# Attention, MLP and experts on one core: the order of steps where the MLP ends and the experts begin

## Chip, core and metric

The kernel runs on one core of a Trainium2 chip. The metric is device time in microseconds of one execution; lower is better. The numbers of before are three timed executions and one execution taken by the hardware profiler.

## What is computed

A gated linear attention over 4 batches, 8 heads, 768 steps and 48 columns a head gives 3072 tokens of 384 columns. An MLP with a hidden layer of 2048 follows, and then eight experts with a hidden layer of 1024, of which each token goes to the one with the largest logit.

```python
def _attn_ref(q, k, v, f_logit):
    f = 1.0 / (1.0 + np.exp(-f_logit))
    for t in range(S):
        state = f[:, :, t, :, None] * state + np.einsum('bhd,bhe->bhde', k[:, :, t], v[:, :, t])
        y[:, :, t] = np.einsum('bhd,bhde->bhe', q[:, :, t], state)

def _moe_ref(x, w_in, w_out):
    h = x @ w_in
    return (h * (1.0 / (1.0 + np.exp(-h)))) @ w_out

def _moe2_ref(x, w_gate, w1, w2):
    logits = x @ w_gate
    expert_idx = np.argmax(logits, axis=1)
    ...
    for e in range(E):
        mask = expert_idx == e
        h = np.maximum(x[mask] @ w1[e], 0.0)
        out[mask] = gate_w[mask, None] * (h @ w2[e])
```

## The kernel before

Products in float32 are made of three: each operand is split into a rounded high part (a cast, on ScalarE) and a low part (a subtraction, on VectorE), and high x low, low x high and high x high are added up in PSUM. So every weight is loaded as `w_raw` and split into `w_hi` and `w_lo`, and every activation likewise.

Tokens go in chunks of 128 rows and groups of two or three chunks. The MLP runs 128 steps (a group and one of 16 blocks of the hidden layer); a step computes `ph` (L420 in the profile, as all matmuls), evicts it into `sg` (VectorE, L679), splits that into `gh` and `gl`, and adds to the output `px` two steps later. After a group its rows `x` are turned (`plt`), multiplied with the gate (`plg`), the best expert is picked, its rank in the expert is counted (`pr`), and `route` scatters the rows into the DRAM buffer `xs` by an indirect DMA of GpSimd. Each row of `xs` carries 384 columns, the weight and the token's number.

The experts run in the order of their size, found from the counts. Of the first expert, the first 256 slots are the head: `head_fetch` loads them (`xe_h`) before the last groups are scattered, and `head_start` and `turn` prepare them during the last MLP step. The other 256 slots are the rest (`rest_fetch`, `xe_r`, 128 rows each), which must wait until the last scatter has landed. `up` is one of eight blocks of an expert's first layer (nine matmuls, then an eviction on ScalarE, `hh`, and one on VectorE, `hl`); `down` is the second layer for 128 tokens (24 matmuls of 384 columns) and ends in `store`: ScalarE scales the rows into `o`, the token's numbers are cast to integers (`oi`, L987), and GpSimd scatters the rows to the output by these numbers. A tile of `up` is in one of two PSUM banks for even blocks, in one of three for odd ones.

Between the last MLP step and `moe2`, which runs the rest and then the other seven experts, stands the joint. Its order is the string `TAIL`, a letter for each step: `o` the output product of one of the two last MLP steps, `f` the next of ten fill steps (eight `up` and two `down` of the head), `l` the turn of the last group's rows, `m` its logits, `p` and `r` pick and route, `w` (`preload`) the four loads and eight splits of the second expert's first layer, `g` `rest_fetch`, `k` the final ranking of the experts, `t` the turn of the rest (`pxs_r`), `F` what is left of the fill steps.

TensorE runs in program order throughout. On ScalarE, VectorE and GpSimd what is wrapped in `keep` holds its program order and the rest is placed by a scheduler; SP's loads of weights and rows are kept. Each queue works strictly in the order that results.

Of the kernel before, what the change touches and what calls it, by code (L numbers as in the profile page):

```python
# [71 lines left out]
KACT = 7  # L72
ND = 1
MO = 'oeh'
TAIL = 'ofolfmfpfrffwgfkfftF'
FILL_H = 3
HF0 = 137
FX = 0
# [29 lines left out]
HEAD = 2  # L108
# [6 lines left out]
def kernel(  # L115
# [14 lines left out]
    nc = tc.nc  # L130
    B, H, S, D = q.shape
    NT, DM = out.shape
    DFF = moe_w_in.shape[1]
    E, _, F2 = moe2_w1.shape
    KC = DM // P
    NF = DFF // P
    NF2 = F2 // P
# [24 lines left out]
    def bank(kind, name):  # L162
        return ps.tile([P, 512], F32, tag=kind, name=name, bufs={"h": 2, "x": 3, "a": 3}[kind])
# [83 lines left out]
    def keep(fn):  # L247
        return lambda *a, **k: tc.keep_in_program_order(fn(*a, **k))  # L248
# [442 lines left out]
    def moe_o(g, i):  # L691
        hi, lo = gt.pop((g, i))
        first, last = (0,), (NF - 1,)
        wh, wl = units["out", i // 4]
        if i in first:
            px[g] = [
                spare_bank.pop() if (g, t) == (1, 0) else bank("a" if g == 1 else "x", f"px_{g}_{t}")
                for t in range(sizes[g])
            ]
        for t in range(sizes[g]):  # L700
            o = px[g][t][:, :DM]
            m = slice(t * P, (t + 1) * P)
            pe.matmul(o, hi[:, m], wl[:, i % 4, :], start=i in first, stop=False)
            pe.matmul(o, lo[:, m], wh[:, i % 4, :], start=False, stop=False)
            pe.matmul(o, hi[:, m], wh[:, i % 4, :], start=False, stop=i in last)
        if i in last:
            moe_x2(g, i)
# [20 lines left out]
    def logits_pe(g):  # L728
        for t in range(sizes[g]):
            r = x2[starts[g] + t]  # L730
            pt = bank("a", f"plt_{g}_{t}")
            for c in range(KC):
                pe.transpose(pt[:, c * P : (c + 1) * P], r[:, c * P : (c + 1) * P], ident)
            rt = att.tile([P, KC, P], F32, tag="sg", name=f"rt_{g}_{t}", bufs=SG)
            (keep(nc.scalar.copy) if t % 2 < RT - 1 else nc.vector.tensor_copy)(rt.rearrange("p c t -> p (c t)"), pt[:, :DM])
            rts.append(rt)

    def logits_pe2(g):
        for t, rt in enumerate(rts):
            pl = bank(LB, f"plg_{g}_{t}")  # L740
            for c in range(KC):
                pe.matmul(pl[:, :E], rt[:, c, :], wgc[:, c, :E], start=c == 0, stop=c == KC - 1)
            nc.vector.tensor_copy(lgt[g][:, t, :], pl[:, :E])
# [223 lines left out]

        return total

    def down(it, t):  # L970
        e = it["e"]
        po = bank("x", f"po_{it['nm']}_{t}")
        m = slice(t * P, min((t + 1) * P, it["w"]))
        n = m.stop - m.start
        for i in range(NF2):
            hi, lo = it["g", i]
            wh, wl = units["w2", e, i // 4]
            pe.matmul(po[:n, :DM], hi[:, m], wl[:, i % 4, :], start=i == 0, stop=False)
            pe.matmul(po[:n, :DM], lo[:, m], wh[:, i % 4, :], start=False, stop=False)
            pe.matmul(po[:n, :DM], hi[:, m], wh[:, i % 4, :], start=False, stop=i == NF2 - 1)  # L980
        store(it, t, po, n)

    def store(it, t, po, n):
        r = it["rows"](t)
        o, idx = it["out"](t)
        nc.scalar.activation(o[:n], po[:n, :DM], AF.Copy, scale=r[:n, DM : DM + 1])
        nc.vector.tensor_copy(idx[:n], r[:n, DM + 1 : DM + 2])  # L987
        ins = keep(nc.gpsimd.indirect_dma_start)(
            out=out[:, :], out_offset=bass.IndirectOffsetOnAxis(ap=idx[:n], axis=0),
            in_=o[:n], in_offset=None, bounds_check=NT - 1, oob_is_err=False,  # L990
        )
        tc.declare_no_dep(ins.ins, group="outs", reason="each row of out is written by one token")
        tc.add_to_no_dep_group("outs", ins.ins)
# [15 lines left out]
    items = {}  # L1009
# [326 lines left out]
    for n in range(NCH):  # L1336
        g, r = group_of[n]
# [74 lines left out]
    def queue(early):  # L1412
# [3 lines left out]
        f=lambda n: load_chunk(n, "f"), k=lambda n: load_chunk(n, "k"), q=lambda n: load_chunk(n, "q"),  # L1416
# [43 lines left out]
            fn(*args)  # L1460
    g = NG - 1
    outs = seq[total - LAG :]
    ops = [(up, i) for i in range(NF2)] + [(down, t) for t in range(HEAD)]

    def fill(n):
        for fn, i in ops[:n]:
            fn(items["head"], i)
        del ops[:n]

    def preload():  # L1470
# [1 line left out]
            load_expert_unit(("w1", 1, j), nc.vector)  # L1472

    todo = dict(
        o=lambda: moe_o(*outs.pop(0)), f=lambda: fill(1), F=lambda: fill(len(ops)), l=lambda: logits_pe(g),
        m=lambda: logits_pe2(g), p=lambda: pick(g), r=lambda: route(g), w=preload, k=rank_rest,
        g=rest_fetch, t=lambda: turn(items["rest"]),
    )
    for c in TAIL:
        todo[c]()  # L1480
# [47 lines left out]
```

## Time and profile before

| | us |
|---|---|
| three executions | 815.58, 817.85, 818.96 |
| median | 817.85 |
| profiled execution, device time | 820.14 |
| its span, first to last instruction | 818.4 |
| TensorE busy in the span | 799.3 (98%) |
| VectorE, ScalarE, GpSimd busy | 468.1, 378.7, 62.5 |

The span is what the trace covers; the device time of the same execution also has what lies around it. A matmul's end in the trace is modelled and overlaps the next one's start, so TensorE's busy share says where it stands still, and not how fast it is. A row of a timeline is a start, a duration, an engine, a line, an operation, the tiles (output<-inputs) and a count; in brackets is the idle time before it and what ended it.

### The profile page before, as it was taken

The page shows a single profiled execution, that of the slowest core. Times are in us where ns is not written, and L with a number is a line of the kernel's source. Part 1 is how long each engine was busy: PE and PEld are TensorE (multiplying, and loading weights), DVE is VectorE, ACT ScalarE, POOL GpSimd, SP SyncE. Part 2 cuts the span into 40 slices and gives each one's busy share as a digit, 9 for nine tenths or more (in the row PEclk, how much of TensorE's full clock was granted, in tenths as well). Part 3 has the DMA queues.
Part 4 walks back from the last instruction along what each step waited for, and adds up shares of the span by engine and source line. Part 5 has one row for each costly group of instructions (what it writes and reads, how often), then busy time and mean ns, then how long its engine had stood idle before and what let it go on. Part 6 is the DMA issues. An engine that isn't in the chain of part 4 may idle for free.

```text
span 818.4 us, 15643 instructions
## 1 busy us (share of the span) xinstructions
PE 799.3 (98%) x5831; PEld 750.0 (92%) x5831; DVE 468.1 (57%) x1258; ACT 378.7 (46%) x838; POOL 62.5 (8%) x114
## 2 busy tenths in 40 slices
PE   7999999999999999999999999999999999999996
PEld 4889979989999999999999999999998999989996
DVE  6789986555556556556556556366565335256420
ACT  5465564453453463454435343355464436455421
POOL 2000000002000100100100100001200110110011
PEclk9799999999999999999999999999999999999999
DMA  9566586424233343343443321424281528546500
GB/s 213 152 167 167 167 248 188 109 41 116 77 89 80 102 94 87 98 107 79 108 97 78 98 68 40 136 59 127 67 308 56 175 70 270 170 154 213 173 26 30
DMA packets 173197, 100.34 MB, mean 123 GB/s; under 512 B 115507, under 2 KB 166723, under 8 KB 173110
## 3 DMA queue, kind: packets, MB, share of 16 engines
q1 hardware_dynamic: 168724, 88.56, 39.6%
q0 software_dynamic: 3280, 9.49, 3.1%
q10 hardware_dynamic: 1106, 1.18, 0.4%
q8 instruction: 48, 0.79, 0.4%
q14 instruction: 39, 0.32, 0.1%
HBM read 79.35 MB, written 16.97 MB: 118 GB/s over the span
## 4 chain that ended last, share of the span: by engine, by line
PE 74%; issue 8%; DVE 7%; DMA 6%; ACT 3%; SPq 1%; POOL 1%; POOLq 0%; ACTq 0%; DVEq 0%
PE ph L420 21%; PE px L420 20%; PE po L420 7%; PE p L420 7%; PE py L420 3%; PE sc L420 2%; DMA w_raw<-in_moe_w_dram 2%; DVE out_cv L248 1%; PE pyb L420 1%; PE pl L420 1%; PE pq L425 1%; PE plt L425 1%; PE p_r L420 1%; PE pk L425 1%; PE po_r L420 1%
## 5 line engine op out<-in xcount | busy, mean ns | idle before, releaser
L420 PE MATMUL px<-out_lo,gh 128*128 128x384 f32 x368 | 130.2, 354 | 0.0
L679 DVE SCALAR_TENSOR_TENSOR sg<-se,ph 128x384 f32<-128x384 f32 (+1 forms) x113 | 60.1, 532 | 117.1 <-ACT se L677 116.0
L420 PE MATMUL ph<-xth,in_lo 128*128 128x384 f32 (+1 forms) x384 | 123.9, 323 | 1.0 <-DVE sg L679 0.8
L420 PE MATMUL px<-out_hi,gl 128*128 128x384 f32 x368 | 124.0, 337 | 0.0
L420 PE MATMUL ph<-xth,in_hi 128*128 128x384 f32 (+1 forms) x384 | 123.6, 322 | 0.0
L420 PE MATMUL ph<-xtl,in_hi 128*128 128x384 f32 (+1 forms) x384 | 122.3, 325 | 1.3 <-DVE sg L248 1.2
L420 PE MATMUL px<-out_hi,gh 128*128 128x384 f32 x368 | 123.4, 335 | 0.0
L677 ACT ACTIVATE se<-ph 128x384 f32<-128x384 f32 (+1 forms) x113 | 53.6, 474 | 137.6 <-PE ph L420 132.1
L687 ACT CAST gh<-sg 128x384 fp32r<-128x384 f32 (+1 forms) x113 | 56.4, 499 | 52.6 <-DVE sg L679 49.0
L688 DVE TENSOR_TENSOR gl<-sg,gh 128x384 fp32r<-128x384 f32 (+1 forms) x113 | 60.5, 535 | 25.8 <-ACT gh L687 24.0
L420 PEld LDWEIGHTS ph<-xtl,in_hi 128*128 128x128 f32 x384 | 71.7, 188 | 3.0 <-DVE sg L248 1.9
L420 PEld LDWEIGHTS ph<-xth,in_lo 128*128 128x128 f32 x384 | 72.2, 188 | 1.8 <-DVE sg L679 1.1
L420 PEld LDWEIGHTS ph<-xth,in_hi 128*128 128x128 f32 x384 | 72.1, 188 | 0.0
L420 PEld LDWEIGHTS px<-out_lo,gh 128*128 128x128 f32 x368 | 69.1, 188 | 2.5 <-ACT gh L687 0.6
L420 PEld LDWEIGHTS px<-out_hi,gl 128*128 128x128 f32 x368 | 69.3, 188 | 0.3
L420 PEld LDWEIGHTS px<-out_hi,gh 128*128 128x128 f32 x368 | 69.1, 188 | 0.0
L420 PE MATMUL po<-w_lo,hh 128*128 128x384 f32 (+4 forms) x184 | 62.9, 342 | 0.0
L420 PE MATMUL po<-w_hi,hh 128*128 128x384 f32 (+4 forms) x184 | 61.9, 336 | 0.0
L420 PE MATMUL po<-w_hi,hl 128*128 128x384 f32 (+4 forms) x184 | 61.9, 336 | 0.0
L276 DVE TENSOR_TENSOR w_lo<-w_raw,w_hi 128x384 fp32r<-128x384 f32 x104 | 52.5, 552 | 13.2 <-ACT w_hi L275 13.2
L420 PE MATMUL p<-xsl,w_hi 128*128 128x480 f32 (+6 forms) x168 | 58.4, 347 | 0.0
L420 PE MATMUL p<-xsh,w_hi 128*128 128x480 f32 (+6 forms) x168 | 58.3, 347 | 0.0
(290 smaller groups left out, 1532.5 us busy)
## 6 DMA issues: line engine op xcount, KB each, us to landing
w_raw<-in_moe_w_dram SPq DMA_DIRECT2D x64, 384.0 KB
xs<-big SPq DMA_DIRECT2D x8, 776.0 KB
in_again<-in_moe_w_in_dram SPq DMA_DIRECT2D x16, 384.0 KB
out_again<-in_moe_w_out_dram SPq DMA_DIRECT2D x16, 384.0 KB
in_raw<-in_moe_w_in_dram SPq DMA_DIRECT2D x15, 384.0 KB
xe<-xs SPq DMA_DIRECT2D x7, 776.0 KB
out_raw<-in_moe_w_out_dram SPq DMA_DIRECT2D x14, 384.0 KB
f<-in_f_logit_dram SPq DMA_DIRECT2D x24, 192.0 KB
```

The costliest lines, as they stand in the source:

```text
L248: return lambda *a, **k: tc.keep_in_program_order(fn(*a, **k))
L276: (keep(lo_engine.tensor_sub) if pin else lo_engine.tensor_sub)(lo[:, h], x, hi[:, h].bitcast(F32))
L420: ins = nc.tensor.matmul(*a, **k)
L425: ins = nc.tensor.transpose(*a, **k)
L677: ac.activation(e, ph[:, :GT], AF.Tanh, scale=0.5)
L679: ve.scalar_tensor_tensor(out=t, in0=e, scalar=1.0, in1=ph[:, :GT], op0=ALU.add, op1=ALU.mult)
L687: ac.copy(hi, t)
L688: ve.tensor_sub(lo, t, hi.bitcast(F32))
```

## The change

`store` casts the token numbers on GpSimd (`nc.gpsimd.tensor_copy`) in place of VectorE. `down` can run in two parts: its eight blocks are split in two halves for the head's second tile, the first half is the letter `H` and the second half with the store is `F`, and the fill steps are now nine. `TAIL` goes from `ofolfmfpfrffwgfkfftF` to `ofoflfmfpfrfgfkffHtwF`: one `up` step stands between the last `o` and `l`, the rest's turn `t` stands between `H` and `F`, and `w` goes from before `g` to behind `t`.

```diff
@@ -72,7 +72,7 @@
 KACT = 7
 ND = 1
 MO = 'oeh'
-TAIL = 'ofolfmfpfrffwgfkfftF'
+TAIL = 'ofoflfmfpfrfgfkffHtwF'
 FILL_H = 3
 HF0 = 137
 FX = 0
@@ -967,24 +967,27 @@
 
         return total
 
-    def down(it, t):
+    def down(it, t, steps=range(NF2)):
         e = it["e"]
-        po = bank("x", f"po_{it['nm']}_{t}")
+        if steps[0] == 0:
+            it["po", t] = bank("x", f"po_{it['nm']}_{t}")
+        po = it["po", t]
         m = slice(t * P, min((t + 1) * P, it["w"]))
         n = m.stop - m.start
-        for i in range(NF2):
+        for i in steps:
             hi, lo = it["g", i]
             wh, wl = units["w2", e, i // 4]
             pe.matmul(po[:n, :DM], hi[:, m], wl[:, i % 4, :], start=i == 0, stop=False)
             pe.matmul(po[:n, :DM], lo[:, m], wh[:, i % 4, :], start=False, stop=False)
             pe.matmul(po[:n, :DM], hi[:, m], wh[:, i % 4, :], start=False, stop=i == NF2 - 1)
-        store(it, t, po, n)
+        if steps[-1] == NF2 - 1:
+            store(it, t, po, n)
 
     def store(it, t, po, n):
         r = it["rows"](t)
         o, idx = it["out"](t)
         nc.scalar.activation(o[:n], po[:n, :DM], AF.Copy, scale=r[:n, DM : DM + 1])
-        nc.vector.tensor_copy(idx[:n], r[:n, DM + 1 : DM + 2])
+        nc.gpsimd.tensor_copy(idx[:n], r[:n, DM + 1 : DM + 2])
         ins = keep(nc.gpsimd.indirect_dma_start)(
             out=out[:, :], out_offset=bass.IndirectOffsetOnAxis(ap=idx[:n], axis=0),
             in_=o[:n], in_offset=None, bounds_check=NT - 1, oob_is_err=False,
@@ -1460,7 +1463,7 @@
             fn(*args)
     g = NG - 1
     outs = seq[total - LAG :]
-    ops = [(up, i) for i in range(NF2)] + [(down, t) for t in range(HEAD)]
+    ops = [(up, i) for i in range(NF2)] + [(down, t) for t in range(HEAD - 1)]
 
     def fill(n):
         for fn, i in ops[:n]:
@@ -1472,7 +1475,8 @@
             load_expert_unit(("w1", 1, j), nc.vector)
 
     todo = dict(
-        o=lambda: moe_o(*outs.pop(0)), f=lambda: fill(1), F=lambda: fill(len(ops)), l=lambda: logits_pe(g),
+        o=lambda: moe_o(*outs.pop(0)), f=lambda: fill(1), H=lambda: down(items["head"], HEAD - 1, range(NF2 // 2)),
+        F=lambda: down(items["head"], HEAD - 1, range(NF2 // 2, NF2)), l=lambda: logits_pe(g),
         m=lambda: logits_pe2(g), p=lambda: pick(g), r=lambda: route(g), w=preload, k=rank_rest,
         g=rest_fetch, t=lambda: turn(items["rest"]),
     )
```

VectorE during the last three-chunk group's last steps, difference (`sg` and `gl` are the MLP's evictions, `oi_h` the head's token numbers):

```order
 L649 TENSOR_TENSOR xtl_6298<-y_6592,xth_6297 128x384
 L688 TENSOR_TENSOR gl_13_6680<-sg_13_6669,gh_13_6679 128x384
-L987 CAST oi_h_7568<-xe_h 128x1
-L987 CAST oi_h_7615<-xe_h 128x1
 L679 SCALAR_TENSOR_TENSOR sg_14_6704<-se_14_6702,ph_14_6692 128x384
 L688 TENSOR_TENSOR gl_14_6707<-sg_14_6704,gh_14_6706 128x384
```

The two casts have left VectorE's queue; on GpSimd they now stand ahead of the scatter of chunks 19 to 21.

SP at the joint, before (`w_1` are the second expert's weights):

```order
L248 DMA w_1_1_raw_7490<-in_moe_w_dram 128x3x256
L248 ISA
L248 DMA xe_r_7496<-xs 128x388
L248 ISA
L248 DMA xe_r_7497<-xs 128x388
L1489 TENSOR_LOAD flag_i
```

SP at the same place, now:

```order
L248 DMA xe_r_7469<-xs 128x388
L248 ISA
L248 DMA w_1_0_raw_7576<-in_moe_w_dram 128x3x256
L248 ISA
L248 DMA w_1_0_raw_7582<-in_moe_w_dram 128x3x256
L248 ISA
L248 DMA w_1_1_raw_7590<-in_moe_w_dram 128x3x256
L248 ISA
L248 DMA w_1_1_raw_7596<-in_moe_w_dram 128x3x256
L1493 TENSOR_LOAD flag_i
```

All four loads of `w_1` have moved behind both loads of `xe_r`.

ScalarE at the joint, before (`hh_h` are evictions of the head's `up`, `o_h` of its `down`):

```order
L947 ACTIVATE hh_h<-p_h_7456 128x256
L248 CAST w_1_0_hi<-w_1_0_raw_7470 128x384 x2
L248 CAST w_1_0_hi<-w_1_0_raw_7476 128x384 x2
L248 CAST w_1_1_hi<-w_1_1_raw_7484 128x384 x2
L248 CAST w_1_1_hi<-w_1_1_raw_7490 128x384 x2
L947 ACTIVATE hh_h<-p_h_7501 128x256
L947 ACTIVATE hh_h<-p_h_7530 128x256
L986 ACTIVATE o_h_7567<-po_h_7542,xe_h 128x384
```

ScalarE at the joint, now (`x_r` is the turned rest, `hh_r` the evictions of its `up`):

```order
L933 CAST x_r<-pxs_r_7569 128x256
L248 CAST w_1_0_hi<-w_1_0_raw_7576 128x384 x2
L248 CAST w_1_0_hi<-w_1_0_raw_7582 128x384 x2
L248 CAST w_1_1_hi<-w_1_1_raw_7590 128x384 x2
L989 ACTIVATE o_h_7614<-po_h_7546,xe_h 128x384
L248 CAST w_1_1_hi<-w_1_1_raw_7596 128x384 x2
L947 ACTIVATE hh_r_7634<-p_r_7688 128x256
L947 ACTIVATE hh_r_7636<-p_r_7702 128x256
```

The eight casts stood ahead of the head's last two `up` evictions; now they stand behind the rest's turn, six of them ahead of the head's second store and all ahead of the rest's `up` evictions. VectorE's eight subtractions have moved in the same way.

## Rows read from the trace of the kernel before

**Rows 1.** stage table: us, then busy us of each engine, granted clock, DMA

```profile
626.00:811.00 185.00, 185.00 (x1070) 177.04 (x1068) 73.19 (x163) 77.99 (x182) 23.39 (x24) 1.00 0.43 142
```

**Rows 2.** TensorE's waits in the whole span: total us, times, longest us

```profile
PE ph L420 <- DVE sg L679: 0.8, 1, 0.8
...
PE plt L425 <- DVE x L721: 0.4, 1, 0.4
PE pxs_r L425 <- DMA xe_r<-xs: 0.4, 2, 0.2
...
PE po_h L420 <- DVE ep_h L948: 0.3, 1, 0.3
```

**Rows 3.** timeline of TensorE before the last MLP group: start us, us, engine, operation

```profile
525.98 0.34 PE L420 MATMUL px<-out_hi,gl 128*128 128x384 f32 x1
526.15 0.33 PE L420 MATMUL px<-out_hi,gh 128*128 128x384 f32 x1
527.25 0.38 PE L420 MATMUL ph<-xth,in_lo 128*128 128x256 f32 x1 [0.76 <-DVE sg L679]
```

**Rows 4.** chain of work that ended last: start us, us, what

```profile
522.65 3.84 DMA xe_h<-xs
...
569.96 1.06 PE p_h L420 x9
...
589.66 8.81 PE p_r L420 x72
...
736.10 5.63 DMA w_raw<-in_moe_w_dram
```

**Rows 5.** timeline of VectorE before the last MLP group

```profile
526.52 0.21 DVE L987 CAST oi_h<-xe_h 128x1 int32<-128x1 f32 x2 [1.94 <-DMA xe_h<-xs]
526.65 0.55 DVE L679 SCALAR_TENSOR_TENSOR sg<-se,ph 128x384 f32<-128x384 f32 x1
```

**Rows 6.** timeline of TensorE before the last logits turn

```profile
568.12 0.34 PE L420 MATMUL px<-out_hi,gh 128*128 128x384 f32 x1
568.88 1.08 PE L425 MATMUL plt<-ident,x 128*128 128x128 f32 x6 [0.42 <-DVE x L721]
```

**Rows 7.** timeline of VectorE at the same place

```profile
568.81 0.55 DVE L721 TENSOR_SCALAR x<-px 128x384 f32<-128x384 f32 x1
```

**Rows 8.** timeline of TensorE at the head's second layer and the rest's turn

```profile
581.88 0.34 PE L420 MATMUL po_h<-w_lo,hh_h 128*128 128x384 f32 x1
582.50 0.44 PE L420 MATMUL po_h<-w_hi,ep_h 128*128 128x384 f32 x1 [0.27 <-DVE ep_h L948]
...
583.30 0.33 PE L420 MATMUL po_h<-w_hi,hh_h 128*128 128x384 f32 x1
583.82 0.33 PE L425 MATMUL pxs_r<-ident,xe_r 128*128 128x128 f32 x1 [0.20 <-DMA xe_r<-xs]
584.36 0.77 PE L425 MATMUL pxs_r<-ident,xe_r 128*128 128x128 f32 x5 [0.21 <-DMA xe_r<-xs]
```

**Rows 9.** timeline of ScalarE from the split to the rest's first layer

```profile
577.12 3.40 ACT L248 CAST w_hi<-w_raw 128x384 fp32r<-128x384 f32 x8
...
589.44 0.58 ACT L986 ACTIVATE o_h<-po_h,xe_h 128x384 f32<-128x384 f32 x1 [3.79 <-PE po_h L420]
...
593.22 0.66 ACT L947 ACTIVATE hh_r<-p_r 128x256 fp32r<-128x256 f32 x2 [1.88 <-DMA out_dram<-o_h,oi_h]
```

**Rows 10.** one-column operations: VectorE's casts (min/median/max ns), GpSimd's subtractions (mean ns)

```profile
L987 DVE CAST oi<-xe x25: 131/153/156, 596.0 to 790.6; 128x1 int32<-128x1 f32 x19, 96x1 int32<-96x1 f32 x1, 48x1 int32<-48x1 f32 x1, 32x1 int32<-32x1 f32 x1
...
L1395 POOL TENSOR_TENSOR big<-out_lo 128x1 fp32r<-128x1 f32 x4 | 1.3, 328 | 22.2 <-DMA xs<-big 13.0 <-DVE qpad L248 4.9 <-DVE out_cv L248 4.2
```

**Rows 11.** timeline of SP's DMA issues

```profile
581.37 0.91 SPq L248 DMA_DIRECT2D xe_r<-xs  x2
...
592.01 2.25 SPq L248 DMA_DIRECT2D w_raw<-in_moe_w_dram  x4
```

**Rows 12.** timeline of VectorE in the rest's first layer

```profile
593.63 0.76 DVE L948 SCALAR_TENSOR_TENSOR hl_r<-p_r,hh_r 128x256 fp32r<-128x256 f32 x2 [1.84 <-ACT hh_r L947]
```

## Prediction

> **What bounds the kernel now.** I read the stage table first: in the long stretch of the experts TensorE is busy for all of its time, at full granted clock [rows 1]. A change can win only where TensorE stands still, and the list of its waits over the whole span has four entries that the change can touch [rows 2]; the others lie in the opening. That list counts from the modelled end of a matmul, which lies after the point at which the next one could start, so I size each stall by starts instead: from the last start before the gap to the first behind it, less the usual pitch (0.17 us for 384 columns, from the first two starts of [rows 3]; nine products of 256 columns take 1.06 us [rows 4]).
>
> - Stall a, before the last MLP group: starts at 526.15 and 527.25 [rows 3], 1.10 - 0.17 = **0.93 us**. VectorE was in the two casts of row numbers, which had waited for the 388 KB of `xe_h`; the `sg` that TensorE needs stood behind them [rows 5].
> - Stall b, before the last logits turn: 568.12 to 568.88 [rows 6], 0.76 - 0.17 = **0.59 us**, for VectorE's eviction of `x` [rows 7].
> - Stall c, in head tile 0's second layer: 581.88 to 582.50 [rows 8], 0.62 - 0.17 = **0.45 us**. The last `up` steps' evictions stood behind the eight casts of the second expert's split, 3.40 us of ScalarE [rows 9], and behind its eight subtractions on VectorE.
> - Stall d, at the turn of the other rows: 583.30 to 583.82 and 583.82 to 584.36 [rows 8], less pitches of 0.17 and 0.09: **0.35 + 0.45 = 0.80 us**, for the two halves of `xe_r`.
>
> Together 0.93 + 0.59 + 0.45 + 0.80 = **2.77 us**, 0.34% of the span. This is the ceiling of what the named stalls can give. The change removes no matmul.
>
> **The change, part by part.**
>
> *Row numbers on GpSimd.* 29 casts leave VectorE (two for the head, two for the rest, 25 for the other experts), a median of 153 ns each [rows 10]. VectorE is not the bound, so their time is worth nothing; their waits are. Stall a goes whole: the `sg` behind them needs nothing of `xe_h`, and VectorE had been idle before the cast for 1.94 us [rows 5], over twice the stall. In its place on GpSimd the two casts stand ahead of the scatter of rows 19 to 21, which the trace has long after 526, so nobody behind them waits. The price of one cast on GpSimd is not in the trace; the nearest row is its 128x1 subtraction, 328 ns [rows 10], with two inputs where the cast has one. At 29 x 0.33 = 9.6 us it lies beside 818 us in which GpSimd mostly waits. In the experts a cast now can stand ahead of an output store and wait for an older store's buffer. Nothing on TensorE waits for these stores within its slack, so I cost that at 0, at most 29 x 0.33 us if every one were exposed, which the full busy time in [rows 1] excludes. Gain: **0.93 us**, floor 0.
>
> [...]
>
> *A step ahead of the logits turn.* One `up` step (1.06 us) now stands between the last product of the MLP and the turn. The second `x` eviction ends at 568.81 + 0.55 = 569.36 [rows 7]; the turn would start at 568.12 + 0.17 + 1.06 = 569.35, and its first three transposes need only the first `x`. Stall b goes: **0.59 us**. But all of the routing behind it starts 569.35 - 568.88 = 0.47 us later, since the number of steps between turn, logits and ranks is unchanged. So the two halves of `xe_r` land 0.47 us later, at 584.29 and 584.83 (their old times are the two starts of [rows 8] that waited for them).
>
> *The other rows' turn amid a product.* One fill step less now stands behind the ranks and half a product more: 12 matmuls x 0.175 = 2.09 us. From 568.29 to the turn TensorE needed 583.82 - 568.29 = 15.53 us, of which 0.59 + 0.45 + 0.35 = 1.39 was standing; the work is 14.14, plus 2.09 is 16.23: the turn comes at 584.52. The first half is there; the second transpose would start at 584.61 and waits until 584.83. Of stall d 0.22 us stay: gain **0.58 us**, between 0.80 if the halves land half a microsecond earlier and 0 if they land as much later.
>
> *Second expert's split behind it.* Stall c goes with it, since nothing is left ahead of the last `up` evictions: **0.45 us**. Here lies the price. SP's queue is in order, so the four loads of the second expert's first layer no longer go out before 567 us but behind `xe_r`, which waits for the scatter. `xe_r` was issued from 581.37 to 582.28 [rows 11]; 0.47 later is 582.75. At the 0.63 us from issue to issue of such loads (four in 2.25 us with 0.37 for the last [rows 11]) they go at 582.9, 583.5, 584.2 and 584.8. What is queued behind: on ScalarE the casts of these loads stand ahead of the second head store's eviction (`o_h`; only the last two casts behind it) and of all evictions `hh_r` of the rest's first layer; on SP the second expert's rows.
>
> When does TensorE notice? Its first `p_r` product moves from 589.66 to 589.66 - 1.62 = 588.04 (b, c and d without a); the eight take 8.81 us, 1.10 each [rows 4]. The banks go round in two rings, and the seventh, at 588.04 + 6 x 1.10 = 594.64, needs that of the third. In the trace the third's eviction ended at 593.63 + 0.76 = 594.39 [rows 12], 1.17 after ScalarE's `hh_r` at 593.22, which waited for the second head store [rows 9]; that is 3.20 us after `o_h` ended at 589.44 + 0.58 = 590.02. After the change `o_h` starts two casts (0.85) behind the third load. Third load + 0.85 + 0.58 + 3.20 + 1.17 = third load + 5.80 us, which must not pass 594.64: **the third load has to land by 588.84**, 4.64 us after its issue. For the time to landing I have 3.84 us of `xe_h`, of the same size, and 5.63 us of a weight load in the busy expert stage [rows 4]. I take the first, because the DMA engines carry little else at 583 to 589: 584.2 + 3.84 = 588.0, no wait, **0 us**. With the second it lands at 589.8 and costs 1.0 us. A load that landed early would give no gain, as TensorE has nothing left to win there.
>
> A page bears on that choice: the Trainium skill, SBUF — State Buffer, section "The DMA setup-cost knee", gives a fixed 2 us plus the bytes at 436 GB/s, an estimate of 2.9 us for 393 KB. The row of `xe_h` is 0.9 us above that. By the page the third load lands at 587.1, the sum stays, and the second rival below would be half as likely.
>
> **Sum.** 0.93 + 0.59 + 0.58 + 0.45 - 0 = 2.55 us, rounded to 2.5. The profiled span of 818.4 becomes 815.9; that execution took 820.14 us, 1.74 around the span, so it becomes 817.6. It lay 2.29 above the median of the three runs, so I take the gain from the median: 817.85 - 2.5 = **815.3 us**.
>
> **Rivals.**
>
> 1. *Loads land late, in part.* At 5.63 us the third load costs 1.0 us and the gain is 1.5: 816.3 us. For it: four loads in a row share the rings with `xe_r` and a head store. Against: the engines are otherwise idle there.
> 2. *Slower.* ScalarE is held by its casts for longer than all gains, and each microsecond past 588.84 costs one. It decides from a third load at 588.84 + 2.55 = 591.4, 7.2 us after its issue; a load of twice 5.63 us would land at 595.5, and the kernel would take 817.85 - 2.55 + 6.7 = 822.0 us. No row shows such a landing on quiet engines.
> 3. *The cast's move does nothing.* If TensorE at 526 also waits for something else as late (`xtl`, or the eviction before), stall a stays: gain 1.6, 816.2 us. Against it: VectorE went straight from the cast into the `sg` [rows 5].
> 4. *More than named.* VectorE and ScalarE have fewer interruptions, and small stalls hidden under modelled ends go too: gain over 4.1, 813.5 us or less. Against: no such wait is listed for the 185 us of the experts [rows 1].
>
> **How the numbers follow.** Forecast 0.60, rival 1 0.20, rival 2 0.05, rival 3 0.08, rival 4 0.07. The three runs shown lie from 2.3 below to 1.1 above their median, so a median of a few runs can be over 1 us off. Range: downwards the ceiling (0.25 more) and 2.0 of spread, 813.0; upwards rival 1 (816.3) and 1.7 of spread, 818.0. It leaves out rival 2 and most of rival 4, some 2 in 10 with the tails. Half a percent, about what a measurement of this kernel can tell from no change, is 4.1 us: the forecast and rivals 1 and 3 lie inside it. Faster: rival 4 with some of the forecast's tail, 0.11. Slower: rival 2 without the part that ends nearer, 0.04. Same: 0.85.
>
> **What would show it.** In the profile after: no wait of TensorE for `sg` near 526 and none for `x` ahead of the logits turn; the last `po_h` row without a wait for `ep_h`; of the turn's two waits for `xe_r` only one of about 0.2 us; `p_r` beginning 2.5 us earlier and running its 72 products without a hole. A hole in `p_r` behind ScalarE's casts, with the casts waiting for `w_raw`, means that the loads were mis-timed, and its length is what to take from the sum. A wait of TensorE near 526 on anything means that stall a had a second cause. A GpSimd cast ahead of an output store that makes ScalarE wait for `o`, and TensorE for its bank, would overturn the first part.

## The result: about half a percent slower, and the profile after

The changed kernel took 820.8 us, the median of 20 runs, and the kernel before 815.6 us, the median of 20 too: a ratio of 1.0052, interval 1.0032 to 1.0072. The forecast was 815.3 us, range 813.0 to 818.0; the measured time lies outside it.

The opening, which the change does not touch, takes a few us more or less from one execution to the next: the first `plt` product starts at 143.5 to 155.0 us in the 17 profiled executions of this document. So I count from that product, the first start in these rows of the operations on that tile (kernel before, then after; min/median/max ns, first and last start):

```profile
L425 PE MATMUL plt<-ident,x x72: 270/272/330, 149.2 to 569.7; 128*128 128x128 f32 x72
```
```profile
L425 PE MATMUL plt<-ident,x x72: 270/272/330, 147.8 to 567.6; 128*128 128x128 f32 x72
```

| us, profiled execution | before | after |
|---|---|---|
| first `plt` to first `p_r` | 440.4 | 437.3 |
| first `p_r` to first `po_r` | 9.9 | 17.5 |
| first `po_r` to the end | 218.9 | 218.3 |
| first `plt` to the end | 669.2 | 673.1 |

**Up to `p_r` everything came that was forecast, and a little more.** TensorE after, the places of [rows 3, 6, 8] (start us, us, operation): the first product of the last MLP group starts 0.17 us behind the last `px`, and neither the logits turn nor the turn of the other rows has a wait; from 500 us to `p_r` TensorE's wait list is empty:

```profile
524.85 0.33 PE L420 MATMUL px<-out_hi,gh 128*128 128x384 f32 x1
525.02 0.28 PE L420 MATMUL ph<-xth,in_lo 128*128 128x256 f32 x1
...
567.07 0.82 PE L425 MATMUL plt<-ident,x 128*128 128x128 f32 x6
...
581.87 0.82 PE L425 MATMUL pxs_r<-ident,xe_r 128*128 128x128 f32 x6
```

**Then the rest's first layer gives back 7.6 us.** The wait list of TensorE, which had no entry for `p_r` [rows 2], and the two holes in its timeline (hole 1, then hole 2):

```profile
PE p_r L420 <- DVE hl_r L948: 4.1, 2, 2.2
```
```profile
589.33 0.28 PE L420 MATMUL p_r<-x_r,w_hi 128*128 128x256 f32 x1
591.54 0.58 PE L420 MATMUL p_r<-x_r,w_hi 128*128 128x256 f32 x1 [1.93 <-DVE hl_r L948]
...
595.15 0.28 PE L420 MATMUL p_r<-x_r,w_hi 128*128 128x256 f32 x1
597.61 0.39 PE L420 MATMUL p_r<-x_r,w_hi 128*128 128x256 f32 x1 [2.18 <-DVE hl_r L948]
```

From start to start, less the pitch of 0.12 us, these are 2.09 and 2.34 us; the brackets count from a modelled end and are 0.16 us shorter. ScalarE there, which [rows 9] show before (the bracket is the idle time and what ended it):

```profile
584.42 0.93 ACT L248 CAST w_hi<-w_raw 128x384 fp32r<-128x384 f32 x2 [1.20 <-DMA w_raw<-in_moe_w_dram]
586.65 0.93 ACT L248 CAST w_hi<-w_raw 128x384 fp32r<-128x384 f32 x2 [1.31 <-DMA w_raw<-in_moe_w_dram]
588.28 0.93 ACT L248 CAST w_hi<-w_raw 128x384 fp32r<-128x384 f32 x2 [0.70 <-DMA w_raw<-in_moe_w_dram]
589.12 0.58 ACT L989 ACTIVATE o_h<-po_h,xe_h 128x384 f32<-128x384 f32 x1
589.59 0.91 ACT L248 CAST w_hi<-w_raw 128x384 fp32r<-128x384 f32 x2
590.41 0.38 ACT L947 ACTIVATE hh_r<-p_r 128x256 fp32r<-128x256 f32 x1
596.38 1.49 ACT L947 ACTIVATE hh_r<-p_r 128x256 fp32r<-128x256 f32 x5 [5.59 <-DMA out_dram<-o_h,oi_h]
```

*Hole 1* is the split: three of its four pairs of casts waited for their load, and only then came `hh_r(0)`, and on VectorE `hl_r(0)`, without which the fifth `p_r` has no bank. *Hole 2* is the last of these rows: `hh_r(1)` waited 5.59 us for the head's second store, because it lies in the memory of that store's `o_h` (e5 to e7 show it); the seventh `p_r` needs the bank that `hl_r(2)`, behind `hh_r(1)`, sets free. GpSimd's and SP's queues:

```profile
590.47 1.07 POOL L248 DMA_INDIRECT out_dram<-o_h,oi_h  x1 [8.15 <-issue]
...
596.14 0.18 POOL L990 CAST oi<-xe 128x1 int32<-128x1 f32 x1 [4.30 <-DMA xe<-xs]
```
```profile
580.15 2.26 SPq L248 DMA_DIRECT2D w_raw<-in_moe_w_dram  x4
590.83 0.38 SPq L248 DMA_DIRECT2D xe<-xs  x1
```

The store was issued at 590.47 and the 776 KB of `xe` at 590.83, 0.36 us behind it; GpSimd's cast shows that `xe` had landed by 596.14, and the store by 596.38. Before, the store went out 0.75 us ahead of `xe`, and `hh_r(1)` [rows 9] followed it after 2.93 us:

```profile
590.29 0.97 POOL L248 DMA_INDIRECT out_dram<-o_h,oi_h  x1 [4.80 <-DVE oi_r L987]
591.04 0.39 SPq L248 DMA_DIRECT2D xe<-xs  x1
```

What the queues carried shows the collision (q0 is GpSimd's store, q1 SP's loads: packets, MB, share of the 16 DMA engines). Before, from the store's issue to 592.50, only the store:

```profile
q0 software_dynamic: 48, 0.20, 31.5%
```

After, from the store's issue to 594.80, only the load of `xe`; the store's packets all come from 594.80 to 596.38, among the last of the load's:

```profile
q1 hardware_dynamic: 448, 0.70, 61.6%
```
```profile
q1 hardware_dynamic: 301, 0.44, 74.1%
q0 software_dynamic: 64, 0.20, 30.8%
```

The rest of the 7.6 us is the clock. The stage table (us, busy us of PE, PEld, DVE, ACT and POOL, granted clock, DMA share, GB/s):

```profile
588.00:590.00 2.00, 1.61 (x14) 1.40 (x12) 1.50 (x5) 1.72 (x5) 0.00 (x0) 1.00 0.09 32
590.00:592.00 2.00, 0.46 (x2) 0.46 (x3) 1.36 (x3) 0.79 (x3) 1.38 (x3) 0.87 0.24 8
592.00:594.00 2.00, 2.00 (x11) 2.00 (x11) 0.00 (x0) 0.00 (x0) 0.00 (x0) 0.50 0.68 183
594.00:596.00 2.00, 1.43 (x9) 1.22 (x7) 0.00 (x0) 0.00 (x0) 0.00 (x0) 0.77 1.04 398
...
598.00:600.00 2.00, 2.00 (x13) 2.00 (x13) 0.77 (x3) 0.64 (x2) 0.00 (x0) 0.58 0.78 290
```

Behind each hole the granted clock falls to its lower level (0.50, that is 1.2 GHz) for some 3 us. From 591.54 to 595.15 TensorE took 3.6 us for 17 steps of 0.12 us, 2.0 at the full clock, and from the seventh `p_r` at 597.61 to the first `po_r` at 602.57 it took 5.0 us instead of 3.3: 3.2 us together. 2.09 + 2.34 + 3.2 = 7.6 us, the loss of the table. That counts where TensorE lost time, not what each cause is worth: the seventh `p_r` started when `hh_r(1)` had been let go, 6.0 us later behind the first `p_r` than before (12.56 against 6.56), whatever hole 1 and the lower clock behind it took ahead of that. On top came only the 1.6 us of the clock behind hole 2.

### The profile page after: what moved, and what is told of

It reads as the page before. It is cut to its first block, busy times and chain, and to the rows that moved or that the text cites. A ratio compares the mean times of both kernels' runs of the same rounds, so it can differ in the third digit from the quotient of the medians.

```text
span 820.9 us, 15670 instructions
## 1 busy us (share of the span) xinstructions
PE 799.9 (97%) x5831; PEld 751.7 (92%) x5831; DVE 464.8 (57%) x1229; ACT 379.2 (46%) x838; POOL 68.1 (8%) x143
## 4 chain that ended last, share of the span: by engine, by line
PE 81%; DVE 7%; DMA 4%; issue 3%; ACT 3%; SPq 2%; POOL 0%; POOLq 0%; ACTq 0%; DVEq 0%
PE ph L420 21%; PE px L420 20%; PE po L420 12%; PE p L420 11%; PE py L420 3%; PE sc L420 2%; DVE out_cv L248 2%; PE pyb L420 1%; DVE in_cv L248 1%; PE pxs L425 1%; PE p_h L420 1%; PE pl L420 1%; PE po_r L420 1%; PE pq L425 1%; PE plt L425 1%
## 5 line engine op out<-in xcount | busy, mean ns | idle before, releaser
L948 DVE SCALAR_TENSOR_TENSOR hl<-p,hh 128x480 fp32r<-128x480 f32 (+6 forms) x56 | 32.4, 579 | 97.2 <-ACT hh L947 97.2
L420 PE MATMUL po<-w_hi,hh 128*128 128x384 f32 (+4 forms) x184 | 61.9, 336 | 0.0
L420 PE MATMUL po<-w_hi,hl 128*128 128x384 f32 (+4 forms) x184 | 61.9, 336 | 0.0
```

The costliest lines, as they stand in the source:

```text
L420: ins = nc.tensor.matmul(*a, **k)
L948: nc.vector.scalar_tensor_tensor(out=lo, in0=ph[:, :w], scalar=0.0, in1=hi.bitcast(F32), op0=ALU.max, op1=ALU.subtract)
```

## The experiments

Each ran five rounds beside the kernel before. The four columns of us are from the one profiled execution of each, counted behind the opening; kernels that are the same up to `p_r` differ by up to 0.9 us there (before and e10; after, e5, e8 and e9). The ratio, with its interval, is of whole times and has the opening's noise in it. In e5 and e14 it says 2 to 3 us more of loss than the columns do; why stays open. Holes are given as TensorE's wait list has them.

| kernel | `plt` to `p_r` | `p_r` to `po_r` | `po_r` to end | `plt` to end | ratio (interval) |
|---|---|---|---|---|---|
| before | 440.4 | 9.9 | 218.9 | 669.2 | 1 |
| after | 437.3 | 17.5 | 218.3 | 673.1 | 1.0052 (1.0032 to 1.0072) |
| e1 | 439.6 | 11.4 | 218.6 | 669.6 | 0.9991 (0.9968 to 1.0014) |
| e2 | 441.5 | 14.4 | 218.6 | 674.4 | 1.0066 (1.0042 to 1.0091) |
| e3 | 437.6 | 12.8 | 218.4 | 668.9 | 1.0005 (0.9987 to 1.0024) |
| e4 | 439.1 | 11.5 | 218.3 | 668.8 | 1.0007 (0.9989 to 1.0025) |
| e5 | 438.1 | 11.8 | 219.7 | 669.6 | 1.0031 (1.0004 to 1.0058) |
| e6 | 439.0 | 9.9 | 219.5 | 668.4 | 0.9987 (0.9973 to 1.0002) |
| e7 | 437.5 | 9.9 | 219.6 | 667.0 | 0.9984 (0.9961 to 1.0007) |
| e8 | 437.8 | 15.7 | 219.9 | 673.4 | 1.0028 (1.0009 to 1.0047) |
| e9 | 438.1 | 14.3 | 218.8 | 671.2 | 1.0021 (0.9992 to 1.0051) |
| e10 | 441.3 | 9.9 | 219.7 | 670.9 | 1.0012 (0.9980 to 1.0043) |
| e11 | 440.0 | 11.5 | 218.5 | 670.0 | 1.0007 (0.9974 to 1.0040) |
| e12 | 437.4 | 9.9 | 220.8 | 668.1 | 0.9998 (0.9968 to 1.0028) |
| e13 | 437.2 | 10.9 | 220.0 | 668.1 | 0.9981 (0.9963 to 1.0000) |
| e14 | 438.4 | 14.5 | 217.9 | 670.8 | 1.0056 (1.0030 to 1.0083) |
| e15 | 437.4 | 10.2 | 218.7 | 666.3 | 0.9958 (0.9945 to 0.9972) |

### First four: undo one part, or do one alone

**e1, the split's letter, with its loads, back to its old place:**

```diff
-TAIL = 'ofoflfmfpfrfgfkffHtwF'
+TAIL = 'ofoflfmfpfrfwgfkffHtF'
```

> The changed kernel with one letter of its order moved: the four loads and eight splits of the second expert's first-layer weights (w) stand ahead of the rest's loads (g) again, as before the change; the other three edits stay. Theory 1 (the moved loads land late, ScalarE runs the splits late, the rest's first layer p_r waits for its evictions and for the head's second store): p_r runs without the two holes of 1.93 and 2.18 us and at the full granted clock, p_r to po_r about 9.9 us as before instead of 17.5; the eviction of ep_h waits behind splits again (0.45 us); the other gains stay (0.93 + 0.59 + some of 0.58), so 813.5 us, ratio to the kernel before 0.9975. Rival 2 (the casts on GpSimd delay the store and so hh_r(1)): the hole before the seventh p_r stays, at least 2 us, and the time is 817 to 819 us. Rival 3 (the split of the head's second product into halves costs): also not below 816.

**e2, the kernel before with the split and its loads alone moved:**

```diff
-TAIL = 'ofolfmfpfrffwgfkfftF'
+TAIL = 'ofolfmfpfrffgfkfftwF'
```

> The kernel before with nothing but w moved behind the rest's turn. Theory 1: the loss of p_r appears in full, about 7.6 us less the 0.45 (ep_h) and 0.58 (xe_r) that the move gives, so 821 to 823 us, ratio 1.008; two holes in p_r before its fifth and seventh step, granted clock at the lower level behind them. Rival 2 (cast on GpSimd): 815 us, as before, and no hole before the seventh p_r.

**e3, the loads ahead of the rest's loads, the splits left behind:**

```diff
-TAIL = 'ofoflfmfpfrfgfkffHtwF'
+TAIL = 'ofoflfmfpfrfWgfkffHtwF'
...
+    def early_loads():              # W
+        for j in range(2):
+            for p in range(2):
+                fetch_half(("w1", 1, j), p)
...
     def preload():                  # w
         for j in range(2):
-            load_expert_unit(("w1", 1, j), nc.vector)
+            for h in range(4):
+                split_half(("w1", 1, j), h, nc.vector)
```

> The changed kernel with the four loads of w put ahead of the rest's loads and the eight splits left where the change puts them, behind the rest's turn: the splits' place on ScalarE and VectorE stays, the landing does not. Theory 1 in the form 'the landing is the cost': the splits start right behind the rest's last x_r cast near 585 and run without a wait on a load, o_h follows by 588, hl_r(0) comes in time, no hole in p_r longer than 0.5 us: 813 to 815 us. Rival 3 ('the place of the splits ahead of o_h and of the evictions is the cost, whenever they land'): eight casts and eight subtractions still hold both engines for 3.5 to 4 us right when p_r needs them, a hole of 1 us or more stays and the time is 817 to 820 us.

**e4, the cast of row numbers back on VectorE:**

```diff
-        nc.gpsimd.tensor_copy(idx[:n], r[:n, DM + 1 : DM + 2])
+        nc.vector.tensor_copy(idx[:n], r[:n, DM + 1 : DM + 2])
```

> The changed kernel with the cast of the row numbers back on VectorE, everything else as changed. Theory 1: the holes in p_r stay and the 0.93 us at 526 comes back, so 821.5 us, ratio 1.0065. Rival 2 (the casts of oi_r on GpSimd and their waits delay the head's second store, and with it hh_r(1)): the store starts 0.5 us or more earlier after o_h, the hole before the seventh p_r shrinks by at least 1 us, and the time is 818 to 819 us although the stall at 526 is back.

Measured: 815.75, 823.54, 816.63 and 816.54 us (before: 816.25). The move of the split alone brings the whole loss (e2), as theory 1 has it. But its profile missed what theory 1 expected: there is no hole before the fifth `p_r`, only one of 2.6 us before the seventh. And the late loads are not the whole cause: with the split's loads back (e1, e3), hole 1 is gone and a hole before the seventh `p_r` stays, 1.2 and 2.7 us, where I had expected 0.5 us at the most. And putting only the casts back (e4) was worth 3.7 us by the ratios (1.0052 to 1.0007) where theory 1 expected a loss of 0.7. In e4 a hole of 1.3 us before the fifth `p_r` is left, hole 2 is gone, and store to `hh_r(1)` is 2.91 us. So there are two mechanisms; the second hangs on the cast, and on the split too (e2).

### Next four: the wait for the store

**e5, e6, e7: the memory of the late tiles handed out in another order**, in the changed kernel, in e1 and in e3. `hh_r(1)` then lies on memory that was free long before:

```diff
-MO = 'oeh'
+MO = 'hoe'
```

> The changed kernel with the memory of the late tiles handed out in another order (hh, o, xe instead of o, xe, hh), so that the rest's second hidden tile hh_r(1) no longer lies where the head's second output o_h lay and does not wait for its store; nothing else is moved. Theory 4 (the loss behind the seventh p_r is that wait: the store's packets queue with the load of xe issued 0.36 us behind it and land 5.8 us later): the wait of hh_r on the store is gone from ScalarE, hole 2 (2.18 us) is gone, hole 1 before the fifth p_r (1.93 us, loads of w_1 late) stays, p_r to po_r falls from 17.5 us to 12 to 14, and the time from 820.8 to 816 to 818 us. Rival 3 (late splits alone): p_r to po_r stays over 16 us, 820 us.

> The kernel of e1_w_ahead (w ahead of the rest's loads again) with the memory order of e5_no_gate. Theory 4: the wait of 1.2 us before a p_r in e1_w_ahead goes, p_r to po_r falls from 11.4 us to 9.9 as before the change, and the time is 1.4 us under e1_w_ahead, 814.3 us, ratio to the kernel before 0.9975. Rival 7 (the time of p_r is set by ScalarE and VectorE whatever the store does): as e1_w_ahead, 815.7 us.

> The kernel of e3_loads_early (loads of w ahead of the rest's loads, splits behind its turn) with the memory order of e5_no_gate. Theory 4: the wait of 2.7 us in p_r goes, p_r to po_r falls from 12.8 us to about 10, and the whole gain of the four edits shows: 813.5 us, ratio 0.997. Rival 3 (splits behind the turn cost by their place): a hole of 1 us or more stays, 815 to 816 us.

**e8, the load of `xe` later, the memory as changed:**

```diff
             r = m2.tile([P, CAP // P, ROW], F32, tag="xe", name=f"xe_{e}", bufs=2)
+            if e == 1:
+                for k in range(2):
+                    late_by = m2.tile([1, E], F32, tag=f"late{k}", name=f"late_{k}")
+                    keep(nc.sync.dma_start)(out=late_by, in_=moe2_w_gate[:1, :])
             keep(nc.sync.dma_start)(out=r, in_=slots_of(e, 0, CAP // P).rearrange("n p d -> p n d"))
```

> The changed kernel with two loads of 8 numbers issued on SP ahead of the load of xe, so that it is issued about 1 us or more later; the memory order is as changed, so hh_r(1) still waits for the head's second store. Theory 4 in the form 'the store lands late because the load of xe is in the queues with it': the store to hh_r(1) falls from 5.9 us to about 2.9, as in the kernel before (where the load was issued 0.75 us behind the store), hole 2 shrinks from 2.18 us to under 0.5, time 817 to 818 us. Rival 8 (the store itself is slow there, from the casts or from its own descriptors): store to hh_r(1) stays at 5 us or more and the time at 820 us.

Measured: 817.76, 815.30, 815.25 and 816.83 us (before: 815.16). With the wait taken away, e6 and e7 have no wait of TensorE in `p_r` and run it in 9.9 us; e5 keeps hole 1 (1.6 us) and nothing else. e7 has no wait of TensorE at all from the last MLP group to `po_r`, so the place of the splits costs nothing once the loads are there (rival 3 of e3 and e7 falls). Their times, 815.3 us, missed the forecasts of 814.3 and 813.5; more on that at e12. e8 decides between theory 4 (the store is late because of the load of `xe`) and rival 8 (it is slow by itself). ScalarE, GpSimd and SP of e8:

```profile
594.62 1.21 ACT L947 ACTIVATE hh_r<-p_r 128x256 fp32r<-128x256 f32 x4 [2.63 <-DMA out_dram<-o_h,oi_h]
```
```profile
591.67 1.07 POOL L248 DMA_INDIRECT out_dram<-o_h,oi_h  x1 [9.24 <-issue]
```
```profile
592.68 0.42 SPq L248 DMA_DIRECT2D xe<-xs  x1
```

With the load 1.01 us behind the store, the same store reaches `hh_r(1)` in 2.95 us. Hole 2 is gone; hole 1 was 2.9 us in that execution (third load 8 us behind its issue), with the lower clock behind it, which is why its profile is no shorter.

### Four more: the clock, the control, the cast alone

**e9, products in the holes:**

```diff
             for i in range(NF2):
+                if e == 0 and i in (4, 6):
+                    spare = bank("x", f"spare_{i}")
+                    for _ in range(14):
+                        pe.matmul(spare[:, :256], units['w1', 0, 1][0][:, 0, 0, :], it['x'][0][:, 0, :], start=True, stop=True)
                 up(it, i)
```

> The changed kernel with 14 products of 128x256 whose result nobody reads put ahead of the fifth and of the seventh p_r, about 1.7 us of TensorE each, inside the two holes. Theory 5 (the lower granted clock behind the holes costs 2 to 3 us of its own): the granted clock stays at 1.00 between 590 and 604, p_r steps behind the holes take 1.1 us again, and the time falls from 820.8 to 818 us although both holes stay. Rival (the clock is not what costs): 820.8 us or, where the products outlast a hole, more.

**e10, the kernel before with `MO = 'hoe'`; e11, the kernel before with the cast on GpSimd and nothing else; e12, e3 with `MO = 'ohe'`:**

> The kernel before with the memory order of e5_no_gate alone. Theory 4: in the kernel before, the store landed in time (2.9 us), so taking hh_r(1)'s wait away gains nothing: p_r to po_r stays at 9.9 us, 815.2 us, ratio 1.000. Rival (the memory order itself is worth something, and e6 and e7 gained by that): ratio 0.998 or less.

> The kernel before with the cast on GpSimd alone, no other edit. Theory 4: the store starts 0.77 us behind o_h instead of 0.27, so that the load of xe is issued 0.25 us behind it instead of 0.75; the store then lands with that load, 5.5 us or more instead of 2.9 to hh_r(1), p_r gets a hole of 1.5 to 2 us before its seventh step, which eats the 0.93 us gained at 526: 816 us, ratio 1.0010. Rival (the cast's move is worth the stall it takes away): 814.2 us, ratio 0.9989, no hole in p_r.

> The changed kernel with the loads of w ahead of the rest's loads (as e3_loads_early) and the late tiles' memory handed out as o, hh, xe, another order in which hh_r(1) does not lie on the head's output. Theory 4: like e7_early_no_gate, no wait of TensorE from the last group of the MLP to po_r, p_r to po_r 9.9 us, 813.6 us, ratio 0.998. Rival (e7 won by something else in its memory order): a hole in p_r, 815 to 816 us.

Measured: 818.42, 817.93, 816.71 and 814.72 us (before: 816.70). In e9 the granted clock was 1.00 through all of `p_r`, and `p_r` to `po_r` fell from 17.5 to 14.3 us, 3.7 of them the added products. That these kept the clock up is not shown: in e3 it stayed at 1.00 behind a hole of 2.7 us without them; and the loads landed a microsecond earlier in that execution. What the clock costs, e3 shows beside e14 (below), with a hole of 2.7 us in the same place: from the seventh `p_r` to `po_r` 3.4 us at 1.00 and 5.0 us where it fell, 1.6 us. e11 is the clearest: the cast alone, which takes the stall at 526 away, makes a hole of 1.4 us in `p_r`. In its profile `p_r` took 1.6 us more, and the times show no gain. GpSimd, SP and ScalarE of e11:

```profile
584.67 0.97 POOL L248 DMA_INDIRECT out_dram<-o_h,oi_h  x1 [4.95 <-issue]
```
```profile
584.97 0.39 SPq L248 DMA_DIRECT2D xe<-xs  x1
```
```profile
590.34 1.49 ACT L947 ACTIVATE hh_r<-p_r 128x256 fp32r<-128x256 f32 x5 [5.11 <-DMA out_dram<-o_h,oi_h]
```

e10 gained nothing, so taking the wait away helps only where there is a collision. e12 has no hole either, but it and all kernels with another memory order lose 1 to 2 us behind `po_r` (219.5 to 220.8 against 217.9 to 218.9). TensorE never waits there; its products are slower. Second-layer products of the experts (busy us, mean ns), e10, then e12:

```profile
L420 PE MATMUL po<-w_hi,hl 128*128 128x384 f32 (+4 forms) x184 | 62.0, 337 | 0.0
```
```profile
L420 PE MATMUL po<-w_hi,hl 128*128 128x384 f32 (+4 forms) x184 | 62.2, 338 | 0.0
```

In the kernel before and after it is 61.9 us, 336 ns; from start to start the mean is 0.1738 us before, 0.1752 in e10 and 0.1763 in e12 (starts less than 0.2 us apart), over 552 products 0.8 and 1.4 us.

### Three more: what was still open

**e13, e3 with the two small loads of e8; e14, e3 with the cast on VectorE.**

> The kernel of e3_loads_early (loads of w ahead of the rest's loads) with the two loads of 8 numbers ahead of the load of xe, as in e8_xe_later; the memory order is as changed, so hh_r(1) waits for the head's second store. Theory 4: the load of xe comes 1 us or more behind the store, the store to hh_r(1) takes 2.9 us, no hole over 0.3 us is left in p_r, p_r to po_r is 9.9 us, and without the slower second-layer products that the other memory orders brought (338 ns instead of 336, 552 of them) from the first plt to the end it is 666.5 us (669.2 in the kernel before, 668.9 in e3_loads_early): 813.2 us, ratio 0.997. Rival 8 (the store is slow by itself): a hole of 2 us or more, 816.5 us, as e3_loads_early.

> The kernel of e3_loads_early with the cast back on VectorE. Theory 4 in the form 'the cast on GpSimd makes the store 0.5 us later and lets the load of xe catch it': the store starts 0.27 us behind o_h again, the load of xe 0.7 us or more behind the store, the store to hh_r(1) takes 2.9 us, no hole over 0.3 us in p_r, 9.9 us from p_r to po_r; the 0.93 us at 526 comes back: from the first plt to the end 667.5 us, 814.5 us, ratio 0.9985. Rival (the gap between the store and the load is not what decides): the hole of 2.7 us of e3_loads_early stays and the time is 817.5 us.

**e15, e3 with one small load into the first words of `xe`, which shifts no tile:**

```diff
             r = m2.tile([P, CAP // P, ROW], F32, tag="xe", name=f"xe_{e}", bufs=2)
+            if e == 1:
+                keep(nc.sync.dma_start)(out=r[:1, 0, :E], in_=moe2_w_gate[:1, :])
```

> The kernel of e3_loads_early with one load of 8 numbers into the first words of xe ahead of the load of xe itself, which has to wait until the 8 numbers have landed: xe comes 2 us or so later than in e3_loads_early, and no tile's place in SBUF moves. Theory 4 with the finding on the places (the first-layer products of the later experts took 349 ns instead of 347 in e8 and e13, whose two small tiles shifted what lies behind them, 504 products): the store to hh_r(1) takes 2.9 us, no hole over 0.3 us in p_r, p_r to po_r 9.9 us, from po_r to the end 218.5 us as in the kernel before (220.0 in e13), so from the first plt to the end 666.3 us against 669.2: 812.8 us, ratio 0.9965. Rival (the 1.1 us behind po_r in e13 came from the later xe, not from the places): 220 us from po_r to the end again and 814.5 us.

Measured: 814.65 and 821.10 us (before: 815.36), and 812.77 us (before: 816.33). e13 came near: the gap from the store to the load was 0.66 us instead of 1, the store took 3.5 us, and a hole of 0.7 us was left. e14 missed: the hole of 2.7 us stayed. The store did start 0.28 us behind `o_h`, but the load came 0.52 us behind the store instead of 0.7 or more. I had taken the 0.7 from the kernel before; VectorE's cast of `flag_i`, on which SP waits ahead of `xe`, starts 0.28 us before `o_h` ends here and in e3, and with its end there. e3's gap of 0.03 and the 0.49 us by which the store is earlier give the 0.52. My forecast of the gap was wrong; that the gap decides was not. GpSimd, SP and ScalarE of e14:

```profile
590.22 1.36 POOL L248 DMA_INDIRECT out_dram<-o_h,oi_h  x1 [5.58 <-ACT hh_r L947]
```
```profile
590.74 0.33 SPq L248 DMA_DIRECT2D xe<-xs  x1
```
```profile
596.22 1.49 ACT L947 ACTIVATE hh_r<-p_r 128x256 fp32r<-128x256 f32 x5 [6.01 <-DMA out_dram<-o_h,oi_h]
```

All executions in which `hh_r(1)` waits for the store, by the gap from its issue to that of `xe`:

| | e3 | e1 | e11 | after | e2 | e14 | e9 | e13 | before | e4 | e8 | e15 |
|---|---|---|---|---|---|---|---|---|---|---|---|---|
| gap, us | 0.03 | 0.30 | 0.30 | 0.36 | 0.47 | 0.52 | 0.53 | 0.66 | 0.75 | 0.82 | 1.01 | 1.05 |
| store to `hh_r(1)`, us | 5.4 | 5.5 | 5.7 | 5.9 | 4.8 | 6.0 | 6.0 | 3.5 | 2.9 | 2.9 | 3.0 | 2.8 |

Up to 0.53 us the store lands amid or behind the load, from 0.66 on it lands by itself. The packets say why. Where the store went first, its first packet came 1.55 to 1.64 us behind its issue; where the load went first, the load's came 0.97 to 1.05 us behind its own. So a load issued less than 1.55 - 1.0 = 0.55 us behind the store begins before it, and the store's packets then came behind 196 (e2) to 483 (e9) of the load's 512. In e1 the row of `hh_r(1)` names `p_r` as what ended the wait, which had long been done; the others name the store. The two groups do not overlap, and four different edits (the cast, the split, the loads, the small loads) put kernels into them.

e15 did what was expected of it: it is 0.4% faster than the kernel before, by an interval clear of 1. ScalarE, GpSimd and SP of e15, and no wait of TensorE from 510 to 640:

```profile
591.57 1.64 ACT L947 ACTIVATE hh_r<-p_r 128x256 fp32r<-128x256 f32 x5 [3.27 <-DMA out_dram<-o_h,oi_h]
```
```profile
588.79 0.97 POOL L248 DMA_INDIRECT out_dram<-o_h,oi_h  x1 [5.67 <-issue]
```
```profile
589.84 0.40 SPq L248 DMA_DIRECT2D xe<-xs  x1
```

It also answers where e13's 1.1 us behind `po_r` went: first-layer products of the experts, e13, then e15 (as before and after):

```profile
L420 PE MATMUL p<-xsh,w_hi 128*128 128x480 f32 (+6 forms) x168 | 58.7, 349 | 0.0
```
```profile
L420 PE MATMUL p<-xsh,w_hi 128*128 128x480 f32 (+6 forms) x168 | 58.3, 347 | 0.0
```

The two small tiles of e13 and e8, eight float32 each, had shifted the tiles behind them by 64 bytes in a partition; e15 has the later load without them and the old pace, so it was the tiles and not the later load that slowed these products. The trace holds no addresses: that the place is what counts is inferred from the edits.

## Why the prediction was wrong, step by step

- *Stalls a, b and c*: right. All three are gone; with the cast on GpSimd the first `p_h` starts 415.8 to 416.8 us behind the first `plt` in twelve executions, with it on VectorE 417.0 to 417.8 in five.
- *Stall d*: forecast 0.22 us left, measured none, since everything before the turn had become quicker. Up to `p_r` the change gained 3.2 us in the profiled pair, where the sum said 2.55; equal kernels differ by up to 0.9 us there, so the sum may be right.
- *The price of the split's move, 0 us*: **this step failed**, in two of its terms. The wait that it priced came to 7.6 us with the cast's share in it, and to 4.5 us in e2, where the split moved alone. First, the time to landing. I took 3.84 us for the third load and allowed 4.64. Its casts started 6.9 us behind its issue (581.4 to 588.28), 5.9 to 8.0 in the other executions where they waited for it (e2, e4, e5, e8). I had priced one load of a queue by a row of one that ran alone, though rival 1 names what is under way with it. The three loads, `xe_r` ahead of them and the head's first store are 1.8 MB; at the 235 GB/s of this stretch that is 7.6 us behind the first issue at 579.0, and it was 9.3. Rival 1, "late in part", named the mechanism; its 5.63 us was still too short. Stage table of the changed kernel:

```profile
579.00:588.00 9.00, 9.00 (x62) 8.44 (x61) 2.91 (x7) 3.36 (x8) 0.97 (x1) 1.00 0.74 235
```

- Second, *the 3.20 us from the end of `o_h` to `hh_r`*, which I carried over from [rows 9] as a constant. It was 590.02 to 593.22 before, and 589.70 to 596.38, 6.7 us, after. It holds only while `xe` is issued late enough behind the store, and I did not price what is queued beside the store, SP's load of `xe` 0.75 us behind it in the kernel before. With the two terms as measured the prediction's own chain for the seventh `p_r` comes out: 588.28 + 0.85 + 0.58 + 6.68 + 1.17 = 597.56, and it started at 597.61. So the path was right, and two durations on it were not.
- *The cast's move*: its gain was right, its cost of 0 was not: alone it cost `p_r` 1.6 us (e11). I looked for GpSimd casts ahead of output stores in the experts, not at the head's second store. With the cast on GpSimd that store starts 0.77 or 0.78 us behind `o_h` in twelve executions, with it on VectorE 0.27 or 0.28 us in five; the 0.5 us are enough to lose the gap (e11).
- *The clock* stood in no term. Behind the seventh `p_r` it brought 1.6 us more.
- *Rival 2* (822.0 us, 0.05) came nearest to the result, but one load was to do it all, landing over 7.2 us behind its issue. At 6.9 us the loads made hole 1 and put `o_h` and its store back; the store's wait and the clock did the rest.

Two pages bear on the failed step. SBUF — State Buffer of the Trainium skill, section "The DMA setup-cost knee", makes an estimate of 2.9 us of one load of 393 KB; behind others in the queue it took 5.9 to 8.0 us here. DMA: Bandwidth & Descriptors of the Trainium skill, section "Queues, rings and completion order", has each DMA engine take turns between the queues, draining a whole packet of about 9 to 17 descriptors, 64 at most, before it turns. If the profile's packets are these descriptors, a load of 512 over 16 engines is 32 an engine, and the store would get its turn behind a quarter to a half of the load, an estimate; it came behind 196 to 483 of the 512, and the wait grew by 1.9 to 3.1 us.

What stays open: why the four loads moved at 235 GB/s, with the DMA engines busy 0.74 of the time, where the loads at 594 to 596 reached 398 at 1.04; and why the granted clock fell behind the holes of the changed kernel, of e2 (2.6 us), e8 (2.9) and e14 (2.7), and not behind that of e3 (2.7). In these four profiled executions it had also fallen in the opening (0.86 to 0.94 from 10 to 70 us), in e3's and in all others with a hole it had not (1.00). Whether that is more than chance was not tried.

## What to carry to other kernels

A duration that ends at a semaphore of a transfer is not a property of the transfer: before you carry it into a sum, list what every queue issues within the same few us, and move that with your edit too. A gain at one place is worth what the next gate lets through; here two buffers sharing memory made the landing of a small store that gate, and an edit that shifted the store against an unrelated load by a few tenths of a us decided more than the stalls it removed. Where run-to-run noise lies in a part that the change doesn't touch, count from a point behind it.

## What the runs showed of the hardware

- A scattered store of 128 rows from GpSimd, issued first, took 2.8 to 3.5 us to its waiter when a 776 KB load on SP's queue came 0.66 us or more behind it, and 4.8 to 6.0 us when it came 0.53 us or less behind. Its first packet comes 1.55 us or more behind its issue, the load's 1.0 us, and the queue that begins second waits for much or all of the other: being issued first by half a microsecond is not enough.
- A store that also waits for GpSimd's own cast started 0.5 us later behind `o_h` than one whose cast ran on VectorE (0.77 against 0.27 us), though that cast had ended some 60 us before. Nothing in the trace shows what the 0.5 us are.
- The pace of products changed with the order of tiles in memory, so presumably with where their operands lie: 349 instead of 347 ns after a shift by 64 bytes, 0.1752 and 0.1763 instead of 0.1738 us from start to start with two other orders of the same tiles. It is 0.8 to 1.4 us of this kernel, and no wait shows it.
- A 128x1 cast took 186 ns on GpSimd and 153 ns on VectorE [rows 10], so the bound of 328 ns from the subtraction was far off. The Trainium skill, GPSIMD Engine Reference, section 4.1, gives about twice as slow for operations with two inputs and roughly line rate for one. The cast has one, and here it is 1.2 times; the subtraction has two.
